# The v of the last batch transposed by DMA inside SBUF, chunk by chunk, instead of by TensorE

**Chip and metric.** One core of a Trainium2 chip. Time is device microseconds of one launch; the median of several runs with the lowest and highest beside it. All runs quoted are of the fast state unless said otherwise. In the traces "us" counts from the start of the span.

## The reference

Cross-covariance attention over four batches (6336 rows, 256 channels), followed by a highway network on each row:

```python
qn = q / (norm(q, axis=1) + 1e-6); kn = k / (norm(k, axis=1) + 1e-6)   # over the 6336 rows
a  = softmax(kn.T @ qn / tau)                                          # 256 x 256 per batch
x  = v @ a
H  = relu(x @ w_h);  T = sigmoid(x @ w_t + b_t)
out = T * H + (1 - T) * x
```

## The kernel before

Per batch there are two stages. Stage 1 streams q and k and accumulates three products in PSUM ("sg": k^T q, k^T k, q^T q). A short chain turns them into a softmax and folds it with the weights into one 256 x 768 matrix ("mr": for x, for h, for t). Stage 2 goes through v in 25 pairs of row tiles (128 rows each; the last pair has 96): v is transposed, and each pair has four matmuls each for "h", "t" and "d" (d = half of relu(h), minus half of x). Stage 1 of the next batch runs beside stage 2 of this one. So the last batch's stage 2 stands alone, at the end.

All loads go through GpSimd's queue (f32 in HBM to f16 in SBUF) and all stores through SyncE's queue, which issues in order. Instructions are put in order by a planner at build time; a task has an engine, a key that ranks it, and the buffers that it takes and drops. v arrives in chunks of 8 row tiles (4 pairs).

TensorE transposes v as 32-bit words, that is two f16 channels at a time, so the channels come out as even and odd ones. For this k is read with a step of two as well:

```python
kc = ka.rearrange("p (w two) -> p two w", two=2)[:, c, :]     # stage 1: k as the stationary operand
...
def transposes(b, i):                                          # two row tiles
    vt_ps[(b, i)] = ps = new("vt", [P, 2, P], f32, ...)        # PSUM
    for u in range(2):
        words = sub("v", b, 2 * i + u).bitcast(f32)
        nc.tensor.transpose(ps[:, u, 0:nr], words, ident0[0:nr, 0:nr])

def evac_vt(b, i, e):                                          # PSUM -> SBUF, on ScalarE or VectorE
    vt = new("vtsb", [P, 2, P], f32, ...)
    copy(e, vt[:, :, 0:nr], vt_ps.pop((b, i))[:, :, 0:nr])
...
seq.append((NP * b + CH // 2 * j - 2, 1, "v", b, j))           # rank of v's loads: 2 pairs ahead
...
tr = plan.add("PE", g - LOOK, ..., take=["vt", "vtsb"], ...)   # in plan_stage2, for each pair g
ev = plan.add(EV, g - LOOK + 0.1, ..., lambda e, i=i: evac_vt(b, i, e))
h  = plan.add("PE", g, ..., [ev] + ready[b] + ...)
...
plan.add("SP", g + 2, 0.1, 0, [y], lambda ...: store(...))     # a store per 4 pairs; 3 output buffers
```

## Time and profile before

| | before |
|---|---|
| time | 283.34 us (283.19 to 283.40, 3 runs) |
| loads end | about 235 us of a span of 281.7 |
| last batch: start of the first h, of the last h | 236.07, 274.63 us |
| two pairs of it | 3.28 us on TensorE |

The prediction shows the lines that this rests on. One more is needed for comparison, that of SyncE's DMA queue; its columns are packets, MB, and the share of the 16 DMA engines' time.

```profile
q1 hardware_dynamic: 4048, 25.95, 23.0%
```

Before the change this queue carries nothing but stores: 4048 packets.

### The profile page before, as it was taken

What the parts mean: (1) busy time and instruction counts of PE and PEld (TensorE: products, weight loads), DVE (VectorE), ACT (ScalarE), POOL (GpSimd) and SP (SyncE); (2) the same over time, 40 slices, a digit from 0 to 9 for tenths busy, and PEclk for the clock granted to TensorE, in tenths of its full rate; (3) what the DMA queues carried; (4) which work ended last, traced back from release to release, by engine and by line L of the source; (5) the groups of instructions that cost most, each with busy time, mean ns of one, the idle gap of its engine ahead of it and who ended that gap; (6) DMA issues with size and microseconds to landing.
All of it is one profiled execution on the core that took longest, in us unless ns stands there. A gap on an engine that the chain in (4) does not pass through costs nothing.

```text
span 281.7 us, 6617 instructions
## 1 busy us (share of the span) xinstructions
PE 258.4 (92%) x2660; PEld 231.8 (82%) x2660; DVE 184.5 (65%) x378; ACT 179.6 (64%) x341; POOL 54.7 (19%) x104
## 2 busy tenths in 40 slices
PE   0797679999999999999999999999999889999992
PEld 0686667999998889999999889999989668888882
DVE  1000035666776886777767977777758968888885
ACT  1000007576777866777777776777766879999992
POOL 7222544221113321111221331111120300000000
PEclk9999999999999999999999999999999999999998
DMA  6999999999999999999999999999999994344434
GB/s 108 214 213 211 212 208 215 212 218 277 282 256 246 286 240 260 270 241 286 266 247 271 285 216 283 259 252 286 269 246 269 286 252 173 121 190 174 183 151 177
DMA packets 16686, 65.57 MB, mean 233 GB/s; under 512 B 1936, under 2 KB 3600, under 8 KB 13712
## 3 DMA queue, kind: packets, MB, share of 16 engines
q0 software_dynamic: 12608, 39.20, 70.4%
q1 hardware_dynamic: 4048, 25.95, 23.0%
q8 instruction: 21, 0.34, 0.4%
q14 instruction: 9, 0.07, 0.1%
HBM read 78.38 MB, written 25.95 MB: 370 GB/s over the span
## 4 chain that ended last, share of the span: by engine, by line
DMA 47%; PE 43%; DVE 3%; POOL 3%; ACT 2%; issue 1%; DVEq 0%; POOLq 0%
DMA k<-in_k_dram 30%; DMA v<-in_v_dram 11%; PE h L625 9%; PE t L625 9%; PE d L625 8%; DMA q<-in_q_dram 6%; PE sg L386 5%; PE vtps L605 4%; PE sg L387 3%; PE sg L388 3%; PE t L656 1%; POOL inv L445 1%; DVE pp L686 1%; ACT d L665 1%; POOL k L284 1%
## 5 line engine op out<-in xcount | busy, mean ns | idle before, releaser
L625 PEld LDWEIGHTS <-vtsb 128*128 128x128 f16 (+1 forms) x1200 | 112.9, 99 | 14.3 <-issue 1.9
L386 PE MATMUL sg<-q,k 128*128 128x256 f16 x384 | 94.0, 276 | 15.8 <-DMA k<-in_k_dram 15.7
L387 PE MATMUL sg<-k 128*128 128x128 f16 x384 | 85.3, 222 | 0.0
L388 PE MATMUL sg<-q 128*128 128x128 f16 x384 | 84.4, 220 | 0.0
L686 DVE SCALAR_TENSOR_TENSOR pp<-uu,d 128x512 f32<-128x512 f32 (+1 forms) x100 | 68.4, 685 | 19.1 <-PE d L625 15.5
L679 ACT ACTIVATE uu<-t 128x512 f32<-128x512 f32 (+1 forms) x100 | 59.8, 599 | 27.5 <-PE t L625 25.6
L665 ACT ACTIVATE d<-h 128x512 f32<-128x512 f32 (+1 forms) x100 | 58.3, 583 | 22.1 <-PE h L625 21.8
L705 DVE SCALAR_TENSOR_TENSOR o<-h,pp 128x512 f32<-128x512 f32 x96 | 66.1, 689 | 2.5
L625 PE MATMUL d<-mr,vtsb 128*128 128x256 f16 (+1 forms) x400 | 59.8, 272 | 0.1
L625 PE MATMUL t<-mr,vtsb 128*128 128x256 f16 (+1 forms) x400 | 59.8, 272 | 0.1
L625 PE MATMUL h<-mr,vtsb 128*128 128x256 f16 (+1 forms) x400 | 59.8, 272 | 0.0
L386 PEld LDWEIGHTS <-k 128*128 128x128 f16 x384 | 37.8, 99 | 18.9 <-DMA k<-in_k_dram 17.4
L400 DVE COPY vtsb<-vtps 128x256 f32<-128x256 f32 (+1 forms) x74 | 31.1, 421 | 26.9 <-PE vtps L605 26.6
L398 ACT COPY t<-bias_all 128x512 f32<-128x512 f32 (+1 forms) x78 | 46.2, 592 | 2.3
L388 PEld LDWEIGHTS <-q 128*128 128x128 f16 x384 | 38.0, 99 | 4.8
L387 PEld LDWEIGHTS <-k 128*128 128x128 f16 x384 | 38.0, 99 | 1.9
L605 PE MATMUL vtps<-ident,v 128*128 128x128 f32 x192 | 36.9, 274 | 1.3 <-ACT vtsb L398 1.1
L434 DVE SCALAR_TENSOR_TENSOR junk<-sg,ident 128x128 f32<-128x128 f32 x16 | 4.6, 288 | 36.9 <-PE sg L388 36.3
L605 PEld LDWEIGHTS vtps<-ident,v 128*128 128x128 f32 x192 | 23.7, 141 | 3.7 <-ACT vtsb L398 1.6
L477 ACT COPY gs<-sg 128x256 f32<-128x256 f32 x8 | 2.6, 377 | 37.8 <-DVE junk L434 37.8
L284 POOL DMA_DIRECT2D k<-in_k_dram x25 | 13.5, 539 | 42.8 <-DMA k<-in_k_dram 16.2
L284 POOL DMA_DIRECT2D v<-in_v_dram x24 | 13.1, 545 | 41.7 <-PE d L625 7.0
(58 smaller groups left out, 118.3 us busy)
## 6 DMA issues: line engine op xcount, KB each, us to landing
out_dram<-o SPq DMA_DIRECT2D x23, 1024.0 KB, 9.0
v<-in_v_dram POOLq DMA_DIRECT2D x24, 512.0 KB, 20.1
q<-in_q_dram POOLq DMA_DIRECT2D x23, 512.0 KB, 21.6
k<-in_k_dram POOLq DMA_DIRECT2D x23, 512.0 KB, 20.6
out_dram<-o SPq DMA_DIRECT2D x2, 512.0 KB, 3.1
out_dram<-ot SPq DMA_DIRECT2D x4, 192.0 KB, 6.2
q<-in_q_dram POOLq DMA_DIRECT2D x2, 256.0 KB, 14.3
k<-in_k_dram POOLq DMA_DIRECT2D x2, 256.0 KB, 11.1
```

The lines of the kernel that those rows point to most:

```text
L284: nc.gpsimd.dma_start(out=t[:, s : s + n, :], in_=main_rows(src)[:, j * CH + s : j * CH + s + n, :])
L386: nc.tensor.matmul(sg[c][:, 0:C], kc, qa, start=first, stop=False)
L387: nc.tensor.matmul(sg[c][:, C : C + P], kc, kc, start=False, stop=False)
L388: nc.tensor.matmul(sg[c][:, C + P : C + 2 * P], qa[:, cs], qa[:, cs], start=False, stop=last)
L398: nc.scalar.copy(out=out, in_=in_)
L400: nc.vector.tensor_copy(out=out, in_=in_)
L605: nc.tensor.transpose(ps[:, u, 0:nr], words, ident0[0:nr, 0:nr])
L625: nc.tensor.matmul(out[0:nr, u, :], vt[u][kt][:, 0:nr], mr[kt][:, col * C : (col + 1) * C], **flags(u, kt))
L665: nc.scalar.activation(out=d[0:nr, :, :], in_=ps_t["h", b, i][0:nr, :, :], func=Act.Relu, scale=0.5)
L679: nc.scalar.activation(out=uu[0:nr, :, :], in_=ps_t.pop(("t", b, i))[0:nr, :, :], func=Act.Tanh, scale=-0.5)
L686: nc.vector.scalar_tensor_tensor(out=pp[0:nr, :, :], in0=el.pop(("uu", b, i))[0:nr, :, :], scalar=1.0, in1=ps_t.pop(("d", b, i))[0:nr, :, ...
L705: nc.vector.scalar_tensor_tensor(out=ot, in0=ps_t.pop(("h", b, i))[0:nr, :, :], scalar=0.0, in1=el.pop(("pp", b, i))[0:nr, :, :], op0=AluO ...
```

## The change

The intent: in the tail TensorE is the bound, and the DMA engines are under half busy there. The transposes of the last batch are moved from the one to the other. The DMA transpose is given f16 elements, so channels come out in natural order, and k of that batch is read in natural order too. `AHEAD` is how many pairs before a chunk's first pair its transpose is ranked; `MOVE` is the size per row tile that the planner assumes for it (its use is cut here). Cut to its core:

```diff
+AHEAD = 8
+MOVE = 100e3
...
-                seq.append((NP * b + CH // 2 * j - 2, 1, "v", b, j))
+                seq.append((NP * b + CH // 2 * j - (10 if b == B - 1 else 2), 1, "v", b, j))
...
+    def by_dma(b):
+        return b == B - 1
...
-            kc = ka.rearrange("p (w two) -> p two w", two=2)[:, c, :]
+            kc = ka[:, cs] if by_dma(b) else ka.rearrange("p (w two) -> p two w", two=2)[:, c, :]
...
+    def transpose_chunk(b, j):
+        vt = new(tag, [P, n, 2, nr], f16, f"{tag}{b}_{j}")           # four such buffers
+        src = tiles[("v", b, j)][0:nr, :, :].rearrange("p s c -> p (s c)")
+        nc.sync.dma_start(out=vt.rearrange("c s kt n -> c (s kt) n"), in_=src, transpose=True)
...
+            if by_dma(b):
+                if 2 * i % CH == 0:
+                    tr = plan.add("SP", g - AHEAD, 0.1, 0, loaded("v", b, 2 * i),
+                                  lambda j=j: transpose_chunk(b, j), take=[vt_tag], ...)
+                ev = tr
+            else:
                 tr = plan.add("PE", g - LOOK, ...)      # as before
                 ev = plan.add(EV, ...)
```

More of the change, by code (lines that the diff above doesn't have):

```diff
@@ L224 @@
         "q": QK_BUFS, "k": QK_BUFS, "v": V_BUFS, "tail_q": 2, "tail_k": 2, "tail_v": 2,
-        "o": 3, "ot": 1, "uu": 3, "pp": 3, "vtsb": 5, "mr0": 2, "mr1": 2,
+        "vT": 4, "vT_t": 1, "o": 3, "ot": 1, "uu": 3, "pp": 3, "vtsb": 5, "mr0": 2, "mr1": 2,
         "sg0": 1, "sg1": 1, "vt": 1, "t": 1, "h": 2, "d": 2,
@@ L230 @@
     pool_of = {tag: psum for tag in ("sg0", "sg1", "vt", "t", "h", "d")}
-    for tag in ("q", "k", "v", "tail_q", "tail_k", "tail_v", "o", "ot"):
+    for tag in ("q", "k", "v", "tail_q", "tail_k", "tail_v", "vT", "vT_t", "o", "ot"):
         pool_of[tag] = stream
@@ L605, in transposes @@
             nc.tensor.transpose(ps[:, u, 0:nr], words, ident0[0:nr, 0:nr])
+    def transpose_chunk(b, j):
+        n = CH if j < NJ else 2
+        nr = P if j < NJ else TR
+        tag = "vT" if j < NJ else "vT_t"
+        vt = new(tag, [P, n, 2, nr], f16, f"{tag}{b}_{j}")
+        src = tiles[("v", b, j)][0:nr, :, :].rearrange("p s c -> p (s c)")
+        nc.sync.dma_start(out=vt.rearrange("c s kt n -> c (s kt) n"), in_=src, transpose=True)
+        for s in range(0, n, 2):
+            vt_sb[(b, (j * CH + s) // 2)] = [[vt[:, s + u, kt, :] for kt in range(2)] for u in range(2)]
     def evac_vt(b, i, e):
@@ L767, in plan_stage2 @@
             g = b * NP + i
-            tr = plan.add(
-                "PE", g - LOOK, 0.22, 0.44, v_deps(g), lambda i=i: transposes(b, i),
-                take=["vt", "vtsb"], drop=drops("v", b, 2 * i + 1),
-            )
-            ev = plan.add(
-                EV, g - LOOK + 0.1, (0.29, 0.35), (0.42, 0.47), [tr],
-                lambda e, i=i: evac_vt(b, i, e), drop=[(tr, "vt")],
-            )
+            if by_dma(b):
+                j = 2 * i // CH
+                vt_tag = "vT" if j < NJ else "vT_t"
+                last_of = i == NP - 1 or (2 * i + 2) % CH == 0
+                if 2 * i % CH == 0:
+                    tr = plan.add(
+                        "SP", g - AHEAD, 0.1, 0, loaded("v", b, 2 * i), lambda j=j: transpose_chunk(b, j),
+                        take=[vt_tag], drop=drops("v", b, min(2 * i + CH, NS) - 1),
+                        size=MOVE * (CH if j < NJ else 2),
+                    )
+                ev = tr
+            else:
+                vt_tag, last_of = "vtsb", True
+                tr = plan.add(
+                    "PE", g - LOOK, 0.22, 0.44, v_deps(g), lambda i=i: transposes(b, i),
+                    take=["vt", "vtsb"], drop=drops("v", b, 2 * i + 1),
+                )
+                ev = plan.add(
+                    EV, g - LOOK + 0.1, (0.29, 0.35), (0.42, 0.47), [tr],
+                    lambda e, i=i: evac_vt(b, i, e), drop=[(tr, "vt")],
+                )
             h_bank, t_bank = h_tag(b, i), t_tag(b, i)
@@ L798, in plan_stage2 @@
                 "PE", g + 0.2, 0.43, 0.63, [r, t], lambda i=i: main_x(b, i),
-                drop=[(tr, "vtsb")]
+                drop=([(tr, vt_tag)] if last_of else [])
                 + ([(mr_own[b], "mr0"), (mr_own[b], "mr1")] if i == NP - 1 else []),
```

## The prediction

> **What bounds the kernel now.** I read the page first: the slices, then the costly groups.
>
> ```profile
> span 281.7 us, 6617 instructions
> ...
> PE   0797679999999999999999999999999889999992
> ...
> DMA  6999999999999999999999999999999994344434
> ...
> L400 DVE COPY vtsb<-vtps 128x256 f32<-128x256 f32 (+1 forms) x74 | 31.1, 421 | 26.9 <-PE vtps L605 26.6
> ...
> L605 PE MATMUL vtps<-ident,v 128*128 128x128 f32 x192 | 36.9, 274 | 1.3 <-ACT vtsb L398 1.1
> ```
>
> One slice is 7.04 us. The DMA engines are full for 33 slices, until about 232 us, when the last loads have landed. After that they are under half busy while TensorE is full until the last slice. So the kernel has two parts: one in which loads and TensorE are both near their limits, and a tail after the loads, in which only the rest of the last batch is computed. The change touches the last batch only, so the tail has to be read by itself. I took busy times by stretches, then the waits of 230 to 275 us:
>
> ```profile
> 220.00:230.00 10.00, 8.71 (x67) 6.74 (x67) 8.19 (x21) 7.61 (x20) 0.81 (x2) 1.00 1.05 269
> ...
> 240.00:250.00 10.00, 10.00 (x90) 8.75 (x88) 8.90 (x17) 9.10 (x20) 0.00 (x0) 1.00 0.35 134
> ```
>
> ```profile
> DVE pp L686 <- PE d L625: 5.6, 14, 1.3
> ACT uu L679 <- PE t L625: 3.5, 13, 0.3
> ```
>
> The columns of the first are window, length, busy TensorE, weight loads, VectorE, ScalarE, GpSimd, clock, DMA share and GB/s. In the tail TensorE has no idle time and no row in the waits; VectorE and ScalarE wait for it. Busy TensorE can hide slack because its durations overlap, so I checked the timeline, where the starts tell the true pitch. This is TensorE in two pairs of row tiles ("h" and "t" are the two layers' products for a pair, "d" adds the attention output to half of the relu of h, "vtps" are the transposes of v; each of h, t and d is four matmuls):
>
> ```profile
> 248.50 0.38 PE L605 MATMUL vtps<-ident,v 128*128 128x128 f32 x2
> ...
> 248.72 0.60 PE L625 MATMUL d<-mr,vtsb 128*128 128x256 f16 x4
> ...
> 249.16 0.60 PE L625 MATMUL h<-mr,vtsb 128*128 128x256 f16 x4
> ...
> 249.59 0.38 PE L605 MATMUL vtps<-ident,v 128*128 128x128 f32 x2
> ...
> 249.81 0.38 PE L656 MATMUL t<-btb,row 128*128 128x512 f16 x1
> ...
> 250.03 0.60 PE L625 MATMUL t<-mr,vtsb 128*128 128x256 f16 x4
> ...
> 250.47 0.60 PE L625 MATMUL h<-mr,vtsb 128*128 128x256 f16 x4
> ...
> 250.90 0.60 PE L625 MATMUL d<-mr,vtsb 128*128 128x256 f16 x4
> ...
> 251.34 0.60 PE L625 MATMUL t<-mr,vtsb 128*128 128x256 f16 x4
> ...
> 251.78 0.38 PE L605 MATMUL vtps<-ident,v 128*128 128x128 f32 x2
> ```
>
> From start to start: two transposes 0.22, four products 0.43 to 0.44, the bias row 0.22. The pattern repeats after 251.78 - 248.50 = 3.28 us, and the parts add to it without a gap: 6 x 0.437 + 2 x 0.22 + 0.22 = 3.28. The tail is bound by TensorE issue, nothing else.
>
> **What the Trainium skill says.** "TensorE: Matmul & The Clock Gate", Part 4: PE-mode transpose, gives about 275 ns for a transpose in a kernel. The trace agrees as a duration (274 ns mean), but back to back they cost 0.11 us each, which is the number that counts here. "DMA: Bandwidth & Descriptors", Latency and other measured facts, gives DMA_TRANSPOSE an effective 261 GB/s with a non-contiguous middle dimension and 350 to 400 GB/s when contiguous; this trace has no such DMA. The same page, Issuing engines are not separate DMA queues, says that DMAs from all engines run on the same 16 DMA engines and interleave. The trace agrees: a 1 MB store issued at 206.91 while loads run lands after about 9 us, one issued at 251.30 after 4.3 us. "VectorE: DVE Perf Modes", The three transpose paths, has 390 ns for TensorE and 1309 ns for the DMA crossbar per 128x128; one at a time the DMA is far slower, so the change lives from the batching of 16 such blocks in a DMA and from its early issue.
>
> **The change part by part.** *Removed:* the 25 x 2 transposes of the last batch. In the order of instructions the first of them stands at 233.23 us of the old timeline, in the saturated stretch. 50 x 0.109 = 5.45 us of TensorE, all on the path. Also 25 evacuations of 0.38 us on ScalarE or 0.42 on VectorE, on engines that were waiting; worth nothing by themselves, but needed, since those engines have to follow a faster TensorE.
>
> *Can they follow?* The new order repeats h, d of the pair before, t, with a bias row in every second t: 6 x 0.437 + 0.22 = 2.84 us per two pairs. ScalarE then has two relus, two gates and a bias copy; starts of neighbours without a wait lie 0.49 to 0.53 apart, so about 2.6. VectorE has two products and two results; the result follows its product by 0.71, the next product 0.60 later, so 2 x 1.31 = 2.62. Both fit with about 0.2 us to spare. Following one round by hand with 0.65 to 0.70 us from a product's start on TensorE to its reader, I find the h bank (three of them) free again some 0.25 us before its next use, the relu done 0.25 to 0.6 us before the d that adds to it, and the copy of the bias 0.5 us before its t. So the new period should be 2.84, perhaps 2.9 with small stalls.
>
> *The sum.* From the first h of the last batch (236.07) to the last (274.63) are 24 pairs, 38.56 us. At 2.84 per two they take 34.1, at 2.9 34.8: 3.8 to 4.5 saved. Four transposes stand before 236.07, 0.44 us. Together 4.2 to 4.9. The end after the last h (4 us and the last stores) is the same.
>
> *Added:* seven DMA transposes on the store queue, six of 128 x 2048 two-byte words = 524 KB and a short one. Estimate from the skill's 261 GB/s: 2.0 us of all DMA engines each, perhaps twice that or more while loads run. When they may start and are needed (first h of a chunk, every 4 pairs = 5.7 us): the first waits for its load, about 211; the second stands behind a store issued at 217.5, the third behind one at 227.9, the fourth behind one at about 238. Needed at 236, 242, 247, 253. From then on each is issued behind a store four to eight pairs earlier, near 244, 250, 255, and is needed near 259, 264, 270. Every one has 14 us or more. They are hidden.
>
> *Moved:* v of the last batch is loaded earlier: its first chunk now stands before the short q and k tails. Those landed at 208.95 and 209.49 and are first used at 215.80; one more 1 MB load ahead, about 2.6 us at the loaded rate (landings in this stretch lie 2 to 4.5 us apart), leaves 3 us. No loss. *k in natural order:* the weight load of a strided k and that of a contiguous q both take 99 ns; no gain or loss.
>
> **The rivals.**
> 1. *VectorE or ScalarE becomes the bound.* For it: at 240 to 250 us they are already 89 and 91% busy. Against: those shares include the evacuations, and the pitches above leave room. If every second stage stalled by 0.15 us, the period would be 3.0 and the gain 2.9 us: 280.4.
> 2. *The transposes are late.* The store queue issues in order, so a slow transpose delays both the next chunk and the stores behind it, and with three output buffers then VectorE. Nothing in the trace tells their cost. Up to some 9 us per chunk is hidden; at 14 us the fifth would be some 7 us late and the sixth later: 290 or more.
> 3. *The traffic delays the loads in the full stretch.* Three transposes fall before 235 us. At 2 to 4 us each, the last v loads (landed 233.25 and 235.41) come up to 12 us later; they are not needed before 250. If they hit the q and k tails by more than the 3 us, the softmax chain starts late by the excess: 1 to 3 us, 280 to 281.
> 4. *More than the sum is gained.* TensorE idles about 1.3 us at 220 to 230, but the chain of the softmax makes that and the change doesn't shorten it. With no stall at all the gain is 5.45: 277.9, still inside 2%.
>
> **Range and chances.** Of 4.2 to 4.9 I take the upper end, since every margin that I followed was positive: 283.34 - 4.84 = 278.5 us. Low 277.2 is just past the full sum; high 282.5 holds rivals 1 and 3. A gain of 2% needs 277.67, more than the removed work, so 0.12 for faster. Slower by 2% is 289.0, rival 2 alone: 0.10. Within 2%: 0.78.
>
> **What would show it.** Right: the two-pair pattern of TensorE in the tail repeats every 2.84 to 2.9 us without vtps; the first h of the last batch starts near 235.6; VectorE and ScalarE stay under 95% busy; TensorE waits for no vT; the transposes land in under 9 us each. Wrong: a TensorE wait for the vT DMA (rival 2), waits for the relu or the results over 0.1 us per pair (rival 1), a late first Gram tail or softmax (rival 3). If the time rises although the pattern is short, the loss is ahead of 236 us.

## The result, and the profile after

**279.54 us (279.18 to 280.29, 4 runs) against 283.32 (283.19 to 283.40, 4 runs); ratio 0.987, interval 0.9847 to 0.9893.** Ratios here are the mean time of one kernel's fast runs over that of the other's of the same rounds, so not quite the ratio of the medians quoted.

From the page after:

```profile
span 278.1 us, 6499 instructions
...
PE   0796679999999999999999999999999887999992
...
DMA  6999999999999999999999999999999999999984
...
q1 hardware_dynamic: 16944, 29.20, 31.6%
```

The DMA engines now count as busy to the end. SyncE's queue has 16944 - 4048 = 12896 packets more, for 3.25 MB: 252 bytes each, the transposes.

TensorE in the tail, from the timeline (start, duration):

```profile
250.72 0.60 PE L642 MATMUL h<-mr,vT 128*128 128x256 f16 x4
...
251.16 0.60 PE L642 MATMUL d<-mr,vT 128*128 128x256 f16 x4
...
251.59 0.38 PE L673 MATMUL t<-btb,row 128*128 128x512 f16 x1
...
253.56 0.60 PE L642 MATMUL h<-mr,vT 128*128 128x256 f16 x4
```

From an h to the second next: 253.56 - 250.72 = 2.84 us, where it was 3.28. The transposes are gone and nothing has come in their place; VectorE and ScalarE follow. By the windows, with the columns as in the prediction:

```profile
230.00:240.00 10.00, 8.32 (x74) 7.11 (x72) 7.62 (x13) 7.71 (x15) 0.00 (x0) 1.00 1.22 221
240.00:250.00 10.00, 10.00 (x90) 8.57 (x89) 9.44 (x15) 9.29 (x19) 0.00 (x0) 1.00 1.09 263
```

The second line shows the steady tail. The first shows a hole in TensorE that was not there before. The timeline has it just ahead of the last batch:

```profile
234.31 0.60 PE L642 MATMUL t<-mr,vtsb 128*96 128x256 f16 x4
236.53 0.61 PE L642 MATMUL h<-mr,vT 128*128 128x256 f16 x4 [1.62 <-DMA vT<-v]
```

Four matmuls take 0.44 us, so the h could have started at 234.75; it starts 1.78 us later, when the first chunk's transpose has landed. And this is SyncE's queue in the timeline, with the time that an issue held SyncE as the second column:

```profile
217.49 13.41 SPq L620 DMA_TRANSPOSE vT<-v  x1
230.99 0.52 SPq L736 DMA_DIRECT2D out_dram<-o  x1
231.61 7.09 SPq L620 DMA_TRANSPOSE vT<-v  x1
...
245.00 2.87 SPq L620 DMA_TRANSPOSE vT<-v  x1
```

The first transpose was issued at 217.49, right behind a store at 217.06, held SyncE for 13.4 us, and landed at 236.49: 19 us, of which 8.5 had gone by when that store landed (225.95). The fourth, after the loads, took 2.9 us of SyncE and landed 5.0 us after its issue.

Where the 3.6 us of the span went, from the two traces: from the first h to the last 38.56 became 34.17 us, 4.39 gained; the first h came 0.46 later (236.53 against 236.07); from the last h to the end of the span 7.40 against 7.07, 0.33 lost. 4.39 - 0.46 - 0.33 = 3.60.

My theory after this: the pattern is as predicted, and the part of the gain that is missing is the late first transpose. The rivals: traffic of the transposes that also costs elsewhere, and loads or stores that any earlier transpose would hold up. "First h" and "last h" below are those of the last batch.

### The profile page after: what moved, and what is told of

Read it like the earlier page. It is cut to its first block, busy times and chain, and to the rows that moved or that the text cites. A ratio compares the mean times of both kernels' runs of the same rounds, so it can differ in the third digit from the quotient of the medians.

```text
span 278.1 us, 6499 instructions
## 1 busy us (share of the span) xinstructions
PE 252.8 (91%) x2610; PEld 226.4 (81%) x2610; DVE 181.4 (65%) x366; ACT 175.1 (63%) x328; POOL 54.5 (20%) x104
## 3 DMA queue, kind: packets, MB, share of 16 engines
q1 hardware_dynamic: 16944, 29.20, 31.6%
## 4 chain that ended last, share of the span: by engine, by line
PE 64%; DMA 30%; POOL 2%; DVE 2%; issue 1%; ACT 0%; DVEq 0%; POOLq 0%; ACTq 0%
PE t L642 12%; PE d L642 12%; PE h L642 12%; PE sg L393 10%; DMA v<-in_v_dram 10%; DMA k<-in_k_dram 7%; DMA vT<-v 7%; DMA q<-in_q_dram 6%; PE sg L394 5%; PE sg L395 5%; PE vtps L612 4%; PE t L673 1%; DVE pp L703 1%; POOL q L286 1%; PE ah L551 1%
## 5 line engine op out<-in xcount | busy, mean ns | idle before, releaser
L642 PEld LDWEIGHTS <-vtsb 128*128 128x128 f16 (+1 forms) x900 | 83.4, 99 | 9.8 <-issue 1.9
L642 PE MATMUL d<-mr,vtsb 128*128 128x256 f16 x300 | 44.8, 272 | 0.1
L642 PE MATMUL t<-mr,vtsb 128*128 128x256 f16 x300 | 44.8, 272 | 0.1
L642 PE MATMUL h<-mr,vtsb 128*128 128x256 f16 x300 | 44.8, 272 | 0.0
L407 DVE COPY vtsb<-vtps 128x256 f32<-128x256 f32 (+1 forms) x62 | 26.1, 421 | 26.1 <-PE vtps L612 25.8
L642 PEld LDWEIGHTS <-vT 128*128 128x128 f16 x288 | 28.1, 98 | 6.5 <-DMA vT<-v 1.9
L612 PE MATMUL vtps<-ident,v 128*128 128x128 f32 x144 | 27.7, 274 | 1.8 <-ACT vtsb L405 1.1
L286 POOL DMA_DIRECT2D k<-in_k_dram x25 | 13.4, 537 | 41.1 <-DMA k<-in_k_dram 15.5
## 6 DMA issues: line engine op xcount, KB each, us to landing
k<-in_k_dram POOLq DMA_DIRECT2D x2, 256.0 KB, 11.3
```

What stands on the lines that cost most here:

```text
L286: nc.gpsimd.dma_start(out=t[:, s : s + n, :], in_=main_rows(src)[:, j * CH + s : j * CH + s + n, :])
L407: nc.vector.tensor_copy(out=out, in_=in_)
L642: nc.tensor.matmul(out[0:nr, u, :], vt[u][kt][:, 0:nr], mr[kt][:, col * C : (col + 1) * C], **flags(u, kt))
```

## The experiments

### The two side parts alone

The load order and the k order of the change, with the transposes back on TensorE:

```diff
-            if by_dma(b):
+            if False:
                 j = 2 * i // CH
```

> The change without its DMA transposes: v of the last batch is loaded early and k is read in natural order, but TensorE transposes v and ScalarE or VectorE evacuate it as before (a wrong result on purpose, since the orders of channels no longer agree). Theory: these two parts are worth nothing, 282.9 to 283.7 us, the two-pair pattern again 3.28 us. Rival (reading k in order makes the weight loads or the Gram matmuls shorter, or the moved load delays the Gram tail): more than 0.5 us off.

Measured: 283.36 us (283.19 to 284.01), ratio 1.0005 (0.999 to 1.002). First h 235.75, last 274.31, the same 38.6 us. Both parts are worth nothing. (The comparison with the reference did not call this run wrong although its channels are mixed up; with norms taken over 6336 rows the softmax is nearly flat, so that test cannot see an exchange of channels of v, and does not check their order in the change either.)

### All transposes earlier

```diff
-AHEAD = 8
+AHEAD = 12
```

> Each DMA transpose is issued 4 pairs earlier, so the first stands ahead of the store that is issued at 217.06 us instead of behind it, and starts when its v has landed (about 211 us); the order on all compute engines is unchanged. Theory (the first transpose is late): the first h of the last batch starts at 234.8 us or before instead of 236.53, TensorE has no wait for vT, and the time is 279.54 - 1.8 = 277.7 us. Rival (the missing part of the gain is taken by DMA traffic beside the tail, wherever it falls): 279.5 or, as stores and loads now wait longer behind transposes, slower.

Measured: 278.29 us (278.04 to 279.53), ratio 0.983 (0.9809 to 0.9851). The first transpose was issued at 210.62 and landed at 230.14, again some 19 us (19.5). The first h started at 234.96 without a wait. So the first step of the theory held. But 0.6 us of the expected gain was missing, and the waits of 225 to 275 us show where (the profiled run, 279.3, is the second slowest of the five, so the others may have lost less there):

```profile
DVE o L722 <- DMA out_dram<-o: 1.3, 1, 1.3
...
PE h L642 <- DVE o L722: 0.9, 1, 0.9
```

A store that was now behind more transposes in SyncE's order was issued at 251.48 instead of 247.97 and landed at 256.70 instead of 253.01. VectorE waited for its output buffer until 256.80, and one gap between two h was 2.6 instead of 1.5 us.

### The load of the last chunk in that run, and the stores

In the run with 12 the load of the last full v chunk waited 11.2 us for a buffer that the first transpose was reading, and was issued at 230.7 instead of 219. Three runs took up this and the order of stores.

```diff
# one more v buffer, AHEAD = 12
-V_BUFS = 7
+V_BUFS = 8
```

> All transposes 4 pairs earlier, as in the run with 12, and one more v buffer, so that the load of the last full v chunk does not wait until the first transpose has read its buffer (in that run it was issued at 230.7 us instead of 219). Theory (that late load then ran beside the next transposes and drew them out, and a store behind them made VectorE wait for an output buffer): the load is issued before 222, no wait for an output buffer, 277.8 to 278.2 us and a narrower scatter than 278.04 to 279.53. Rival (the transposes' own traffic and SyncE's order cause the wait): the gap of 2.6 us between two h is still there, 278.3 us or more. A risk beside both: the load now stands before the norm in GpSimd's order and may delay the softmax.

Measured: 280.62 us (279.61 to 282.87), ratio 0.9919 (0.9884 to 0.9954). The load was issued at 212.47, but the first transpose now took 24 us (210.82 to 234.87), held SyncE for 17.9 us, and the output-buffer wait was longer:

```profile
DVE o L722 <- DMA out_dram<-o: 2.1, 1, 2.1
PE h L642 <- DVE o L722: 1.7, 1, 1.7
```

The theory of the late load fell, since the wait stayed without it; what is left is the rival, the transposes' own time and SyncE's order. With more loads beside it the first transpose took longer.

```diff
# only the first transpose earlier
-                        "SP", g - AHEAD, 0.1, 0, ...
+                        "SP", g - (12 if j == 0 else AHEAD), 0.1, 0, ...
```

> Only the first DMA transpose is issued 4 pairs earlier, ahead of the store at 217; the other six stay where the change has them, and the order on every compute engine is unchanged. Theory (the late first transpose is the only loss, and moving the later ones in the run before only delayed stores): first h of the last batch at 234.9, pattern 2.85 us per two pairs throughout, no wait of VectorE for an output buffer, time 277.7 to 278.1 us. Rival (any earlier transpose delays some store or load by as much as it gains): 278.3 or more, with a wait for a store or for a later transpose in the trace.

Measured: 289.29 us (289.09 to 289.85), ratio 1.0217 (1.0204 to 1.0231): slower, in all of five runs. The first h was at 234.81 as expected. But now the second transpose stood behind two stores (issued at 225.83 and 227.48), took from 227.90 to 249.26 to land, and the fifth h waited for it:

```profile
PE h L642 <- DMA vT<-v: 8.7, 1, 8.7
...
240.00:250.00 10.00, 1.34 (x10) 0.84 (x9) 1.59 (x3) 1.09 (x3) 0.00 (x0) 0.68 1.08 143
```

The second line is the window of 240 to 250 us: DMA engines counted as full, yet 143 GB/s. The load issued at 230.59 beside this transpose landed only at 247.75. Both crawled: from 236 to 240 us the trace has 183 packets of the transpose and 43 of loads. Why 21 us here, where the second transpose of the run with 12 took 11.5 (226.53 to 238.03, one store ahead of it) beside the same loads, is not settled.

```diff
# AHEAD = 12, stores of the last batch from GpSimd's queue, ranked behind its loads (cut)
+        queue = nc.gpsimd if by_dma(b) else nc.sync
-            nc.sync.dma_start(out=main_rows(ob)...
+            queue.dma_start(out=main_rows(ob)...
```

> All transposes 4 pairs earlier as in the run with 12, and the stores of the last batch issued by GpSimd, so that no store of it stands behind a transpose in SyncE's order. Theory (the wait of VectorE for an output buffer came from the in-order queue of SyncE): first h at 234.9, no such wait, 277.6 to 278.0 us, perhaps up to 1 us more if the last stores land later from GpSimd. Rival (the DMA engines are short of bandwidth, whoever issues): the wait for the output buffer is still there, 278.3 or more.

Measured: the fast runs 285.26 to 285.54 us, ratio 1.0076 (1.0062 to 1.0091); three of six runs were slow ones of 294.8 to 298.7 and are left out. The part that the theory was about held: no wait for an output buffer, first h at 234.85, last at 270.21, though TensorE now waited 1.0 us in all for two later transposes. The loss is elsewhere: the last store landed at 276.95, but the span ended at 283.8, 6.8 us later; in the change these are 276.69 and 278.1. The trace shows no work in that stretch, only that the chain of waits ends in GpSimd's queue. This run cannot rank the total times.

### What the transposes cost besides

The first form of this run replaced the transposed v by a constant tile:

> No transposes at all in the last batch: TensorE reads a constant tile in place of the transposed v (a wrong result on purpose), so neither lateness nor DMA traffic is left, with the same order of work on every compute engine. Theory (the only loss is the late first transpose): like the change with its 1.8 us of waiting taken off, 277.5 to 277.9 us, pattern 2.84 us. Rival (the traffic of the transposes also slows loads, stores or SBUF accesses): clearly below 277.4.

Measured: 287.31 us (287.01 to 287.94), ratio 1.0143, and it doesn't test what it should. With no reader of v, the planner gave the buffers out again at once; a load then waited for the one before it (GpSimd waited 4.4 us for a v load), GpSimd stood still, and VectorE waited 7.5 us for the norm that stands behind that load in GpSimd's order. The first h came at 244.10. Only its pattern is of use: 2.84 us per two pairs.

The mended form keeps each transpose in its place, with one block of sixteen:

```diff
-        nc.sync.dma_start(out=vt.rearrange("c s kt n -> c (s kt) n"), in_=src, transpose=True)
+        nc.sync.dma_start(out=vt.rearrange(...)[:, 0:1, :], in_=src[:, 0:P], transpose=True)
...                                                       # matmuls read a constant tile
```

> Mended form of the run without traffic: each DMA transpose moves one 128x128 block in place of sixteen, at the same place in the queue, and TensorE reads a constant tile (a wrong result on purpose); the order of loads and of all compute engines is that of the change. Theory (the late first transpose is the only loss): first h at 234.8, 2.84 us per two pairs, 277.5 to 277.9 us. Rival (the traffic costs elsewhere too): below 277.3.

Measured: 278.11 us (277.80 to 278.93), ratio 0.9822 (0.9809 to 0.9834). No wait for vT; the first h to the last took 34.03 us, against 34.17 in the change. The result is the level without lateness and traffic: 0.9822 against 0.987 of the change, a difference of 0.0048, or 1.4 us of 283.3. I had expected 277.5 to 277.9 (its profiled run was its slowest, with stage 1 ending a microsecond later than in the others). This run takes lateness and traffic away together. But from the first h to the last the traffic costs just 0.14 us, and the lateness of the first transpose, 1.78 us in the trace of the change, is enough for all that is missing within the scatter.

### Do the other engines have room?

The change with 23 copies of a PSUM tile put back on ScalarE and VectorE in turn, TensorE's order as in the change but for two transposes that fill that tile once:

```diff
+                if i >= 2:
+                    plan.add(EV[i % 2], g - LOOK + 0.1, 0.01, 0.02, [hs[i - 2]],
+                             lambda i=i: dummy_evac(b, i, EV[i % 2]))      # 128x256 f32, PSUM -> SBUF
```

> The change with 23 copies of 128x256 from PSUM put back on ScalarE and VectorE in turn, one each per two pairs, read by nobody; TensorE's order as in the change. Theory: the evacuations could not have stayed: VectorE would need 2.62 + 0.35 to 0.42 = 3.0 us and ScalarE about 2.6 + 0.38 = 3.0 per two pairs against TensorE's 2.84, so the pattern lengthens to 3.0 to 3.05 us and the time by about 2 us, 281 to 282. Rival (TensorE alone sets the pace and both have room): 279.5 to 279.9.

Measured: 280.06 us (279.91 to 281.05), ratio 0.9891 (0.9874 to 0.9909). The steady gaps between two h became 1.65 and 1.32 us, so 2.97 per two pairs, close to the 3.0 expected; both engines were then nearly full:

```profile
250.00:260.00 10.00, 10.00 (x86) 8.21 (x85) 9.76 (x19) 9.68 (x21) 0.00 (x0) 1.00 1.07 315
```

VectorE went from one copy to the next without a gap:

```profile
249.92 0.41 DVE L407 COPY vtsb<-vtps_d 128x256 f32<-128x256 f32 x1
...
250.25 0.68 DVE L714 SCALAR_TENSOR_TENSOR pp<-uu,d 128x512 f32<-128x512 f32 x1
...
252.89 0.41 DVE L407 COPY vtsb<-vtps_d 128x256 f32<-128x256 f32 x1
```

From start to start the copy takes 250.25 - 249.92 = 0.33 us of a round of 252.89 - 249.92 = 2.97. Without it the round is 2.64, so against TensorE's 2.84 VectorE has 0.20 us to spare.

The time rose less than expected, since the first six gaps kept the short pattern, and the first h was less late in this profile (235.57). With the evacuations VectorE would have become the bound at 2.97. The copies saved are therefore needed for 0.13 of the 0.44 us gained per two pairs. That they save nothing by themselves was not tested.

### What a transpose takes

Each full chunk transposed a second time, into a tile that nobody reads:

```diff
+        vx = new("vX", [P, n, 2, nr], f16, f"vX{b}_{j}")
+        nc.sync.dma_start(out=vx.rearrange("c s kt n -> c (s kt) n"), in_=src, transpose=True)
```

> Every full chunk is transposed twice, the second time into a tile that nobody reads. It measures what a transpose really takes when they are back to back. If the 4.9 us that SyncE spends on one in the tail are the transpose's own rate (descriptors or crossbar), a chunk of four pairs needs 2 x 4.9 + 0.5 = 10.3 us against the 5.7 us of TensorE and the time goes to 290 to 300 us. If most of it is waiting behind the store in front, with 2.9 us as the real cost, a chunk needs about 6.4 us and the time is 281 to 284.

Measured: 293.53 us (two runs, 293.45 and 293.62), ratio 1.0362: within the first of the two ranges, but not for its reason. The first transpose landed at 236.66, much as in the change, and from there one store and two transposes took 5.9 to 9.3 us, 7.9 on average (SyncE's stores were issued at 236.34, 243.99, 252.96 for the short one, 258.88, 268.21 and 275.97). That is neither 10.3 nor 6.4: from the second chunk on, the second transpose, right behind the first, held SyncE for only 1.8 to 3.0 us, so the 4.9 is not a transpose's own rate. Four pairs of TensorE are 5.7 us. So the tail has room for one transpose per chunk and not for two.

I counted the DMA packets of the change in the trace by size: those of 256 bytes are the transposes, those of SyncE's queue above that are the stores, those of GpSimd's queue the loads (its 4-byte packets counted too).

```
window (us)   transpose   store   load packets
222 - 224           0        55        61
224 - 226          25        30        72
226 - 228         110         0       110
228 - 230         189         0       136
230 - 232         299         0        86
232 - 234         472         0        38
234 - 236         953        16         0
236 - 238           0        96         0
238 - 240        1824        16         0
```

A chunk has 2048. Those of the second, after the loads, go from 238.36 to 240.23, which is 281 GB/s; those of the later full chunks take 2.6 to 3.2 us, 201 to 162 GB/s. The first transpose began at 225.47, as the store ahead of it in the same queue came to its end (it landed at 225.95). Until 230 it got about one small packet for each load packet (299 against 246); then the loads thinned out, and they ended at 235. The Trainium skill has such a rule: "DMA: Bandwidth & Descriptors", Queues, rings and completion order, says that each DMA engine takes turns between the queues that have work, a whole packet at a time. The traces agree, most closely where loads last longer beside a transpose: 473 small packets against 472 of loads from 216 to 224 us in the run with 12, 683 against 686 from 216 to 228 with one more v buffer, 1547 against 1544 from 164 to 192 in the run with two batches below. So beside loads a transpose went packet for packet, however small its packets are. The stretch of 183 against 43 packets in the run with only the first transpose earlier does not fit this.

The times of landing say the same more bluntly: a full first transpose landed 1.3 to 2.9 us after the last load in flight, at 236.49 after 235.14 in the change, at 236.66 after 233.76 in the run just above, at 234.87 after 232.21 with one more v buffer, and in the run with 12, whose last load was held back, at 230.14 after 228.76. The small one of the run with one block, 128 packets, needed 11.3 us, of which 8.5 behind its store, and did not wait for the loads to end.

### The first chunk in parts

```diff
# two DMA transposes of four row tiles for the first chunk (in the second run four, of two)
+    def transpose_half(b, k):
+        n = CH // 2
+        vt = new("vT_0", [P, n, 2, P], f16, f"vT_0{b}_{k}")
+        src = tiles[("v", b, 0)][:, n * k : n * k + n, :].rearrange("p s c -> p (s c)")
+        nc.sync.dma_start(out=vt.rearrange("c s kt n -> c (s kt) n"), in_=src, transpose=True)
```

> The first chunk's transpose is cut into two of four row tiles each, at the same place in SyncE's order; nothing else changes. Theory (turns: beside the loads the DMA engines take about one 256-byte packet of the transpose per 4 KB load packet, so a transpose takes time by its number of packets and not by bandwidth): the whole chunk's 2048 packets took from about 224.5 to 236.3 us, the first 1024 of them about 8 of these 12 us, so the first half lands near 232 to 233, before the first h (234.8) needs it, the second half near 236.5, before the third (237.6): no wait of TensorE, 278.0 to 278.3 us. Rival (a transpose beside loads has a long fixed cost or latency, not turns): the first half lands no earlier than 235.5 and the second comes later than before, 279.5 us or more.

Measured: 278.67 us (278.02 to 279.25), ratio 0.9827 (0.9809 to 0.9845). The halves landed at 235.26 and 236.02: the first much later than the 232 to 233 of the theory, but early enough to cut the wait, with the first h at 235.31; so the rival, which had the time at 279.5 or more, did not come true either. No new wait stands behind it. Of the versions with a right result this one and the run with 12 are the fastest; both beat the kernel before, and the change by about 0.4%, though the interval of the run with 12 (up to 0.9851) just overlaps that of the change (from 0.9847). They were not timed against it on one chip.

> The first chunk's transpose in four parts of one pair each, at the same place in SyncE's order. In the run with two halves the first half landed at 235.26 and not at 232 to 233, because only 618 of the 2048 packets had gone by 232 us and 977 by 234. Theory (progress by packets, each part usable when its own are through): the first 512 packets are through at about 231.3, so the first part lands near 232.5, before the first h (234.8), and the second near 235.2, before the second h (236.3): no wait of TensorE for vT, last h at 269.0, 277.8 to 278.1 us, the level of the run with small transposes. Rival (parts in one queue land together when the loads have ended, about 235): the first h still waits 0.5 us, 278.4 to 278.9 us as with halves.

Measured: 279.74 us (279.65 to 280.33), ratio 0.9868 (0.9852 to 0.9885). The rival was right about the landing, but the time is longer than it said. The four parts landed at 235.53, 235.91, 236.41 and 236.84: together, when the loads had ended, although 596 packets of 256 bytes had gone by 232. My picture of "each part is usable when its share of packets is through" fell here; the count over all engines doesn't tell when the slowest of them is through (a likely reason, not tested). The first h came at 235.58, and a later one waited for vT:

```profile
248.24 0.61 PE L650 MATMUL h<-mr,vT 128*128 128x256 f16 x4 [1.15 <-DMA vT<-v]
```

It belongs to the third chunk, whose transpose was issued behind a store at 239.80 and landed at 248.20, after 8.4 us. In the change it stood behind the same store and took 6.5 (239.41 to 245.93). Why it took longer here is not settled.

### The last two batches

```diff
     def by_dma(b):
-        return b == B - 1
+        return b >= B - 2
...                                # and the same for the rank of v's loads
```

> The same change for the last two batches, to see what it costs where the loads fill the DMA engines. Theory (turns and a full DMA): the additional 6.25 chunks run beside loads, each takes 12 to 20 us from issue to landing against 5.7 to 9 us that four pairs take there, and they take DMA time from loads that are at their limit, some 2.5 us of all engines each: at least 10 us slower than the change, 290 us or more. Rival (DMA transposes are hidden wherever they stand and TensorE gains 5.4 us more in the earlier batch): 275 to 278 us.

Measured: 325.45 us (322.68 to 331.3; one of four runs was slow), ratio 1.1445 (1.1398 to 1.1492). The first transposes of the earlier batch took 47 and 49 us from issue to landing (153.88 to 201.00, 178.82 to 227.81). The first of them stood behind a store that landed at 162.60; from there its 2048 packets, one for each load packet, took 38.4 us. From the waits:

```profile
POOL v L286 <- DMA vT<-v: 69.8, 5, 24.7
...
PE h L642 <- DMA vT<-v: 36.8, 3, 22.0
```

GpSimd, which issues all loads in order, stood 70 us behind buffers that a transpose was still reading, and so held back the loads of q and k too. The direction was as expected and the size far beyond it: by the waits it is not the DMA time of the transposes (2.5 us for the packets of a chunk where no loads ran), but the wait of loads for transposes that wait for loads. More v buffers, which would test this, were not tried.

## Why the prediction was right, and where it was not

It was 278.5 us in 277.2 to 282.5, and within 2% at 0.78; measured 279.54, ratio 0.987.

- **The bound, and the sum for it: right.** "6 x 0.437 + 0.22 = 2.84 us per two pairs" was measured as 2.84; "24 pairs ... at 2.84 per two they take 34.1, at 2.9 34.8" was 34.17. Without traffic and lateness the time is 278.11 us, 0.4 below the 278.5 predicted.
- **"Can they follow?": right,** with the "about 0.2 us to spare": 2.97 us with the copy put back, 2.64 without its 0.33.
- **Moved loads and k in natural order, "no loss" and "no gain or loss": right,** 1.0005 alone. (The short k tail landed 4.7 us later, at 214.19, and not 2.6; that was still 2 us before its use at 216.24.)
- **"They are hidden": wrong for the first of seven.** Two terms failed. Its issue, "the first waits for its load, about 211": it stood behind the store of 217.06 in SyncE's order, because I had taken that store's place for the one of the store before; the order of instructions has it, the timeline merges stores. And its time, "2.0 us of all DMA engines each, perhaps twice that or more while loads run": 19 us from issue to landing, 8.5 of them behind that store and 10.5 for its packets, most of that in turns with those of loads, which the estimate from bytes leaves out. It came 1.78 us late. For the transposes after the loads the terms are about right: 1.9 to 3.2 us for the packets of a full chunk against 2.0, landing in 5 to 7 us. So of its signs three failed: no wait for vT, the first h near 235.6 (236.53), every landing under 9 us.
- **The rivals.** Rival 2, late transposes, is what happened, small and at the first chunk, not at the fifth as I had it. Rival 3 did not: the last v loads landed at 232.99 and 235.14, no later than before (233.25 and 235.41), so the loads did not pay; the transpose did. Rival 1 is close by, 0.2 us, but not reached. Rival 4's limit of 277.9 was not passed by any run's median.

## What to carry to other kernels

Taking work off the engine that sets the pace pays just its issue time there (0.109 us a transpose and not its duration of 0.27), if the engines after it can take the faster pace: count their pitches too. A DMA of many small packets that shares the DMA engines with large loads takes time there by its number of packets: here 2048 took 10.5 to 38.4 us from the landing of the store ahead, and 128 took 2.8. Issue it so that nothing needs it before the loads end, or keep it out of loaded stretches. Where one queue issues in order, read the place of the new DMA among the others from the order of instructions, and try moves of it on the chip: each of the earlier places tried here traded one wait for another, from 278.3 to 289.3 us.

## What the Trainium skill lacked or had wrong

- "DMA: Bandwidth & Descriptors", Latency and other measured facts: the 261 GB/s for a DMA transpose is of the right size where no loads run (in the change 162 to 281 GB/s over the packets of a full chunk, stores beside it); beside loads, 19 to 24 us from issue to landing for 0.5 MB, 47 to 49 where loads fill the engines for long. The page has the turns between queues, but no figure for this.
- The same page has no measured time for how long a transpose from SBUF to SBUF holds the issuing queue on this chip (its part on trn3 has only a count of sequencer cycles for "previous generations"): here 1.8 to 5.2 us of SyncE for a full chunk in the quiet tail, 13.4 to 24.2 for the first one beside loads, against 0.3 to 0.5 for most stores.
- "TensorE: Matmul & The Clock Gate", Part 4: PE-mode transpose gives 275 ns in a kernel, which is the duration here (274); its cost back to back is 0.11 us, and that part doesn't say so.
